# A work list recorded first and ordered by the kernel's own scheduler, with fixed buffers, fewer register loads, first transposes on the matrix engine and weight loads held to set steps

## The chip, the cores and the metric

The kernel runs on one core of a Trainium2 chip. A core has five engines that each work through an instruction list of their own, in order: TensorE (PE in the profile, with its weight loads as PEld), VectorE (DVE), ScalarE (ACT), GpSimd (POOL) and SyncE (SP). Here SP computes nothing; it issues the DMA transfers, which 16 DMA engines then carry out. The metric is the device time of one execution in microseconds (us). Before the change its median over three runs is 957.5 us (956.35 to 960.08).

## What is computed

Block-sparse attention over 4 batches, 8 heads, 768 positions and head size 64, followed by a two-layer feed-forward network (FFN) on the 3072 rows that come out. The arithmetic is carried in pairs of fp16 numbers (a high and a low part), so a product takes two or three matmuls.

```
scores = scale * np.matmul(q, k.transpose(0, 1, 3, 2))
# mask: own and neighbouring blocks of 32, first and last block,
#       and 3 sampled blocks for each block of queries
scores = np.where(mask, scores, -1000000000.0)
attn = np.exp(scores - max); attn = attn / (sum + 1e-09)
x = attn @ v                     # heads joined: 3072 x 512
h = x @ w_in                     # 512 x 2048
g = np.maximum(0.01 * h, h)
out = g @ w_out                  # 2048 x 512
```

## The kernel before

The queries of a batch are cut into 12 *tiles* T of 64 rows. Four tiles make an *item* (12 items). Within a tile each pair of heads is a *unit*: 192 units, worked on in 192 *steps* by one Python loop over `units`. The first tile of a batch (T = 0, the first and the last block) sees all 768 keys and has two *parts* for each unit; the others see 384 gathered keys. So there are 208 parts.

A unit goes through: `unit_scores` (PE L628, two query operands qs and qxs for the high and low parts), `unit_ttr` (DVE L637: mask, scale and row minimum), `unit_exp` (ACT L648), `pair_norm` (DVE L656, L657), `unit_high` (ACT L663: high half of the probabilities, pp), `unit_split` (DVE L668: low half; then a DMA transpose of pp into pt, issued on SP at L671), `pair_av` (PE L689: 24 matmuls for two parts). `tile_evac` turns a finished tile into x (ACT L698, DVE L701, ACT L707, POOL L709). When the four tiles of an item are there, its FFN work may start: 192 matmuls h (L724) and 96 matmuls o (L751), with ACT L731, DVE L735 and L740 and POOL L741 between them. The score and av matmuls use the array in another shape than the FFN's: they run as pieces of 128x64, the FFN's matmuls as 128x128.

Keys and queries are prepared by `prep_k` and `prep_q`, which end in DMA transposes on SP (L494, L517). For a tile after the first, `gather_k` copies six sampled key blocks on POOL (L573), each behind a register load (L572), and `gather_v` fetches six sampled value blocks by DMA on SP (L603), each behind a register load on SP (L601).

The weights arrive as 8-byte numbers and are decoded to fp32 and split: `load_w` (SP L286), `decode` (ACT L292, DVE L293 to L298), `finish` (PE L172 and L122, then ACT L353 and L355, POOL L356). They come in eight parts (four quarters of w_in and of w_out). The FFN of the first two items runs quarter by quarter as its weights become ready; all later items wait for the whole.

The order on each engine was made by the framework: the instructions are written in program order with a priority each (`tc.cur_priority`, 200 for each step), tile pools hand out buffers, and the framework's own list scheduler with a timeline model fixes the order. `bank` and `scale_sum` take PSUM banks from pools: two for scores, two for o, three for h and all sums, one for av. `in_order` adds order between the gathers.

Of the kernel before, what the change touches and what calls it, by code (L numbers as in the profile page):

```python
# [11 lines left out]
F16 = mybir.dt.float16  # L12
BF16 = mybir.dt.bfloat16
F32 = mybir.dt.float32
I32 = mybir.dt.int32
# [38 lines left out]
    "v_at": 28,  # L54
    "wr": [(0, 1.0), (4, 3.0), (10, 4.0), (18, 4.5)],
    "wsplit": "ppppppdd",
    "xbufs": 3,
}


@with_exitstack
def tile_block_sparse_attention_ffn(
# [19 lines left out]
    nc = tc.nc  # L82
# [17 lines left out]
    cst = ctx.enter_context(tc.tile_pool(name="cst", bufs=1))  # L100
    pw = ctx.enter_context(tc.tile_pool(name="pw", bufs=1))
    sm = ctx.enter_context(tc.tile_pool(name="sm", bufs=4))
    pa = ctx.enter_context(tc.tile_pool(name="pa", bufs=2))
    pf = ctx.enter_context(tc.tile_pool(name="pf", bufs=2))
    dr = ctx.enter_context(tc.tile_pool(name="dr", bufs=2, space=bass.MemoryType.DRAM))
    ps_s = ctx.enter_context(tc.tile_pool(name="ps_s", bufs=2, space=bass.MemoryType.PSUM))
    ps_o = ctx.enter_context(tc.tile_pool(name="ps_o", bufs=2, space=bass.MemoryType.PSUM))
    ps_1 = ctx.enter_context(tc.tile_pool(name="ps_1", bufs=1, space=bass.MemoryType.PSUM))
# [3 lines left out]

    def bank(name, tag="h"):
        return ps_1.tile([P, 512], F32, tag=tag, name=name, bufs={"h": 3, "av": 1}[tag])

# [32 lines left out]
    loose = set()  # L148

    def scales(ss, n, name, **how):  # L150
        now = tc.cur_priority
        tc.cur_priority = now - CFG["bs"]
        begin = len(nc.cur_bb.bb.instructions)
        pb = scale_sum(ss, n, name)
        loose.update(i.name for i in nc.cur_bb.bb.instructions[begin:])
        r = scale_of(pb, n, name, **how)
        tc.cur_priority = now + 8
        return r

    eye = cst.tile([P, P], BF16, name="eye")  # L160

    def squares(parts, name, fl):


        now = tc.cur_priority
        tc.cur_priority = now - CFG["bs"]
        pb = bank(f"{name}_sq")
        blocks = [t.bitcast(BF16).rearrange("p (n l) -> p n l", l=2)[:, c:c + P, 1]
                  for t in parts for c in range(0, t.shape[1], P)]
        begin = len(nc.cur_bb.bb.instructions)  # L170
        for i, t in enumerate(blocks):
            nc.tensor.matmul(pb[:, :P], t, t, start=(i == 0), stop=(i == len(blocks) - 1))  # L172
        loose.update(i.name for i in nc.cur_bb.bb.instructions[begin:])
# [3 lines left out]
        tc.cur_priority = now + 24  # L177
# [11 lines left out]
    offs = cst.tile([1, NB * NR], I32, name="offs")  # L189
    mask = cst.tile([P, NT - 1, SLOTS], F32, name="mask")  # L190

    def load_constants():
        nc.sync.dma_start(out=eye, in_=c_eye)
        nc.sync.dma_start(out=row, in_=sampled.bitcast(I32).rearrange("(o a) b -> o (a b)", o=1))
# [4 lines left out]
    def build_masks():  # L199
        nc.vector.tensor_scalar(  # L200
            out=offs, in0=row.rearrange("p (a b) -> p a b", b=2)[:, :, 0], scalar1=5, scalar2=None,
            op0=ALU.logical_shift_left)
# [17 lines left out]
        pm = bank("mask_ps")[:, :(NT - 1) * 2 * NR].rearrange("p (t a r) -> p t a r", t=NT - 1, a=2)  # L220
# [56 lines left out]
    def load_w(g):  # L277
# [8 lines left out]
        nc.sync.dma_start(out=raw.rearrange("p (c x) l -> p c (x l)", c=g.w), in_=src.bitcast(I32))  # L286

        def decode():


            lo, hi, f, d = raw[:, :, 0], raw[:, :, 1], g.d, g.d.bitcast(I32)
# [14 lines left out]
    def prep_weights():  # L306
# [33 lines left out]
        def finish(n, kind, gs):  # L340
            inv, s = scales(squares([g.d for g in gs], f"{kind}{n}", "w"), 1, f"{kind}{n}", keep=f"{kind}{n}", fl="w")
# [66 lines left out]
    def prep_v(b):  # L408
# [13 lines left out]
        scr[b] = dr.tile([S, H * 2 * D], F16, tag="scr", name=f"scr_{b}")  # L422
# [44 lines left out]
    def prep_k(b, hp, rk):  # L467

        nm = f"k{b}_{hp}"
# [30 lines left out]
    def prep_q(b, j, i, rq):  # L500

        nm = f"q{b}_{j}_{i}"
# [14 lines left out]
        nc.sync.dma_start_transpose(out=qs, in_=flat(qa))  # L517
# [22 lines left out]
    def in_order(key, begin):  # L540

        new = nc.cur_bb.bb.instructions[begin:]
        last = last_use.setdefault(key, deque())
        if len(last) > 1:
            for i in new[:-1]:
                tc.add_manual_dep(i, last[0], mybir.DependencyInfo(
                    mybir.DependencyClass.NoSync, mybir.DependencyReason.DATA), reason="order")
            last.popleft()
        last.append(new[-1].name)
# [8 lines left out]
    def gather_k(b, T):  # L558
# [11 lines left out]
        for slot, i in sampled_of(T):  # L570
            begin = len(nc.cur_bb.bb.instructions)
            off = nc.gpsimd.value_load(offs[:1, i:i + 1], min_val=0, max_val=S - BLOCK)  # L572
            nc.gpsimd.tensor_copy(  # L573
# [576 lines left out]
```

## Time and profile before

| what | us |
|---|---|
| median of three runs | 957.5 |
| span of the profiled execution | 959.4 |
| TensorE matmul busy | 775.6 (81%) |
| VectorE busy | 609.4 (64%) |
| ScalarE busy | 493.8 (51%) |
| GpSimd busy | 328.3 (34%) |
| mean share of the DMA engines' time | 67.8% |

The profiled execution's own time is its span, from the first to the last instruction; it lies 0.2% above the median of the three runs. Busy time of TensorE counts a matmul from its start to its modelled end, and matmuls overlap, so it overstates the work: 24 h matmuls that follow each other take 24 times the distance of their starts, not 24 times their length. SP's DMA issues are not counted as busy; they are shown as SPq.

### The profile page before, as it was taken

What the parts mean: (1) busy time and instruction counts of PE and PEld (TensorE: products, weight loads), DVE (VectorE), ACT (ScalarE), POOL (GpSimd) and SP (SyncE); (2) the same over time, 40 slices, a digit from 0 to 9 for tenths busy, and PEclk for the clock granted to TensorE, in tenths of its full rate; (3) what the DMA queues carried; (4) which work ended last, traced back from release to release, by engine and by line L of the source; (5) the groups of instructions that cost most, each with busy time, mean ns of one, the idle gap of its engine ahead of it and who ended that gap; (6) DMA issues with size and microseconds to landing.
All of it is one profiled execution on the core that took longest, in us unless ns stands there. A gap on an engine that the chain in (4) does not pass through costs nothing.

```text
span 959.4 us, 21885 instructions
## 1 busy us (share of the span) xinstructions
PE 775.6 (81%) x7020; PEld 485.8 (51%) x7020; DVE 609.4 (64%) x1643; ACT 493.8 (51%) x1061; POOL 328.3 (34%) x469
## 2 busy tenths in 40 slices
PE   1325445878988989997988979897989999999998
PEld 1213233535556555554655545555555655655675
DVE  4986778897576957455766556556666566655221
ACT  4564774755564646445545545555555554545121
POOL 0133544562213424423422344332423334432221
PEclk9996555999998999998999999998998999999999
DMA  9995986957767676685676868766785755556200
GB/s 212 279 269 117 271 169 141 204 113 151 152 167 147 125 147 148 147 146 122 134 175 133 161 121 144 164 135 132 162 164 104 151 135 131 119 114 124 34 23 23
DMA packets 336625, 139.39 MB, mean 145 GB/s; under 512 B 299389, under 2 KB 311678, under 8 KB 336510
## 3 DMA queue, kind: packets, MB, share of 16 engines
q1 hardware_dynamic: 336510, 137.99, 67.8%
q8 instruction: 55, 0.90, 0.4%
q14 instruction: 60, 0.49, 0.2%
HBM read 65.57 MB, written 12.58 MB: 81 GB/s over the span
## 4 chain that ended last, share of the span: by engine, by line
PE 41%; DMA 19%; DVE 16%; SPq 9%; issue 7%; ACT 7%; POOL 0%; ACTq 0%; DVEq 0%
PE h L724 17%; PE o L751 15%; DMA pt<-pp 9%; PE s L628 4%; PE av L689 4%; DVE pp L668 3%; DMA kt<-k_k 3%; DVE p L637 3%; SPq L601 2%; ACT p L648 2%; DMA qs_q<-qa_q 2%; ACT pp L663 2%; SPq L603 2%; SPq L671 2%; DMA W<-in_moe_w_in_dram 1%
## 5 line engine op out<-in xcount | busy, mean ns | idle before, releaser
L724 PE MATMUL h<-x,W 128*128 128x256 f16 x2304 | 288.0, 280 | 1.7 <-DVE k_tot L136 1.2
L751 PE MATMUL o<-W,g 128*128 128x512 f16 x1152 | 280.0, 384 | 4.8 <-DVE g L740 2.7
L724 PEld LDWEIGHTS <-W 128*128 128x128 f16 x2304 | 225.1, 101 | 52.9 <-issue 11.0
L668 DVE SCALAR_TENSOR_TENSOR pp<-p,r,pp 128x384 f16<-128x384 f32 x208 | 151.6, 737 | 128.2 <-ACT pp L663 127.5
L741 POOL TENSOR_TENSOR g<-ht,g 128x512 f16<-128x512 f32 x96 | 115.1, 1199 | 263.6 <-DVE g L740 170.7
L663 ACT ACTIVATE pp<-p,r 128x384 f16<-128x384 f32 x208 | 122.0, 608 | 143.2 <-DMA pt<-pp 111.9
L648 ACT ACTIVATE p<-p,mx 128x384 f32<-128x384 f32 x208 | 126.4, 608 | 98.2 <-DVE mx L637 61.6
L573 POOL COPY kg<-kt 128x256 f16 x264 | 128.5, 508 | 133.9 <-PE s L628 73.2
L751 PEld LDWEIGHTS <-g 128*128 128x128 f16 x1152 | 103.3, 98 | 135.0 <-issue 22.8
L689 PE MATMUL av<-pt,vg 128*64 128x128 f16 x2112 | 100.7, 231 | 47.6 <-DMA pt<-pp 44.8
L637 DVE CUSTOM_DVE_ANT_0 p<-s,em,nsc 128x384 f32<-128x384 f32 x176 | 106.1, 609 | 33.2 <-PE s L628 32.5
L689 PEld LDWEIGHTS <-vg 128*64 128x64 f16 x2112 | 79.5, 115 | 88.8 <-issue 76.4
L735 DVE SCALAR_TENSOR_TENSOR ht<-h,gd,ht 128x512 f32<-128x512 f32 x80 | 59.6, 746 | 54.8 <-ACT ht L731 54.7
L709 POOL TENSOR_TENSOR x<-xf,x 128x256 f16<-128x256 f32 x48 | 34.4, 717 | 155.8 <-ACT x L707 155.8
L731 ACT ACTIVATE ht<-h,gs 128x512 f32<-128x512 f32 x80 | 54.0, 675 | 56.2 <-PE h L724 45.2
L628 PE MATMUL s<-kg,qs_q 128*64 128x384 f16 x352 | 66.4, 368 | 17.9 <-DVE mx L637 15.1
L628 PEld LDWEIGHTS <-qs_q 128*64 128x64 f16 x416 | 27.8, 114 | 92.5 <-issue 70.4
L628 PE MATMUL s<-kg,qxs_q 128*64 128x384 f16 x352 | 63.7, 350 | 6.9 <-DMA qxs_q<-qs_q 6.9
L740 DVE CAST g<-ht 128x512 f16<-128x512 f32 x96 | 41.7, 435 | 8.9 <-PE o L751 7.8
L628 PE MATMUL s<-kt,qs_q 128*64 128x384 f16 x64 | 12.8, 396 | 35.0 <-DVE mx L637 19.7
L648 ACT ACTIVATION_READ_ACCUMULATOR p<-p,mx 128x1 f32 x208 | 39.0, 187 | 0.0
L356 POOL TENSOR_TENSOR W<-W 128x1024 f16<-128x1024 f32 x12 | 28.8, 2409 | 28.5 <-ACT W L355 22.0
(126 smaller groups left out, 727.1 us busy)
## 6 DMA issues: line engine op xcount, KB each, us to landing
vg<-scr SPq DMA_DIRECT2D x280, 64.0 KB, 1.9
vg<-scr SPq DMA_DIRECT2D x44, 256.0 KB, 3.1
v<-in_v_dram SPq DMA_DIRECT2D x32, 192.0 KB, 4.0
qxs_q<-qs_q SPq DMA_DIRECT2D x48, 128.0 KB, 2.4
scr<-v SPq DMA_DIRECT2D x16, 384.0 KB, 3.5
W<-in_moe_w_in_dram SPq DMA_DIRECT2D x5, 1024.0 KB, 7.2
rq<-in_q_dram SPq DMA_DIRECT2D x20, 256.0 KB, 3.9
out_dram<-ob SPq DMA_DIRECT2D x20, 256.0 KB, 2.8
```

The costliest lines, as they stand in the source:

```text
L573: nc.gpsimd.tensor_copy(out=kg[:, :, slot * BLOCK:(slot + 1) * BLOCK], in_=kt[:, :, bass.ds(off, BLOCK)])
L628: nc.tensor.matmul(sp[hh * D:(hh + 1) * D, :], st[:, h, c0:c0 + Q2], keys, start=(n == 0), stop=(n == 1))
L637: nc.vector.tensor_tensor_reduce(out=u.p[i], in0=u.sp[i], in1=kgs[u.b, u.T][1] if u.T else zero.to_broadcast([P, KEYS]), scale=u.nsc, scal ...
L648: nc.scalar.activation(u.p[i], u.p[i], AF.Exp, scale=-1.0, bias=u.mx[:, :1], accum_out=u.pair.sum[:, u.pi, i:i + 1])
L663: nc.scalar.activation(pp[:, 0, :], p, AF.Copy, scale=u.r)
L668: nc.vector.scalar_tensor_tensor(out=pp[:, 1, :], in0=p, scalar=u.r, in1=pp[:, 0, :], op0=ALU.mult, op1=ALU.subtract)
L689: nc.tensor.matmul(pr.av[hh * D:(hh + 1) * D, u.hp], vt[:, l * D:(l + 1) * D], u.pt[c // NCH][:, :, c % NCH, hh * D:(hh + 1) * D], start=( ...
L724: nc.tensor.matmul(c.ph[:, i], W16[:, 2 * b, d, wl, o:o + P], it.x[:, xl, d, :], start=(d == 0 and m == 0), stop=(d == NP - 1 and m == 2))
L731: nc.scalar.activation(c.t, c.ph, AF.Copy, scale=scale[1])
L735: nc.vector.scalar_tensor_tensor(out=c.t, in0=c.ph, scalar=scale[0], in1=c.t, op0=ALU.mult, op1=ALU.max)
L741: nc.gpsimd.tensor_tensor(out=c.g[:, 1], in0=c.t, in1=c.g[:, 0], op=ALU.subtract)
L751: nc.tensor.matmul(it.po[t], c.g[:, gl, i, t * P:(t + 1) * P], W16[:, 2 * (f // PER) + 1, f % PER, wl, :], start=(c.first and i == 0 and m ...
```

## The change

The kernel's calls no longer go to the framework's engines directly. `Plan` and `Engine` stand in their place: each call becomes a `Task` with an engine, a priority, a modelled cost, and the memory cells that it reads and writes. `Plan.block` joins a run of matmuls into one task that is not broken up (12 matmuls of h, 6 of o, 12 of av, 4 of scores for one part). At the end `Plan.order` runs an event model in which every engine takes the ready task with the lowest priority number, PE with a surcharge (`stay`) on a task of another array shape, and `Plan.issue` writes the instructions out in that order for the framework to keep.

Buffers are fixed rings in place of pools (`Pool`, `banks`); sums and squares go to the free last 128 columns of the two score banks (`corner`), so the three h banks hold only h. Three gathered blocks share one register load, and the values are clamped beforehand so that no bounds check stands in the queue. The transposes of the first item (four of keys, two of queries, 20 of probabilities) are done by PE against a unit matrix, with a copy out of PSUM on ACT, four of them on DVE (`turned`). A weight part's load may start only when a given step's exp has begun (`after`, `wp`, `wlead`).

```diff
+    "stay": 400.0,
+    "wp": [2, 5, 14, 17, 20, 23, 26, 29],
+    "wlead": 4,
...
+class Plan:
+    def add(self, t):
+        t.prio, t.n, t.then, t.gate = self.prio, len(self.tasks), [], self.gate
+        self.prio += 1.0
...
+        for i in need:
+            self.tasks[i].then.append(t.n)
...
+        def take(t, e):
...
+            if e == "PE":
+                best = min(ready[e], key=lambda j: tasks[j].prio + (CFG["stay"] if tasks[j].kind != mode[0] else 0.0))
+                ready[e].remove(best)
+            else:
...
+                best = heapq.heappop(ready[e])[1]
...
+    def issue(self):
+        order, self.begun = self.order()
+        with self.tc.manual_schedule():
+            for i in order:
+                for run in self.tasks[i].run:
+                    run()
...
-    nc = tc.nc
+    nc = plan = Plan(tc)
...
+    def corner():
+        buf = spare[turn["sum"] % 2]
...
+        return View(buf.ap[:, KEYS:], buf, buf.gen)
...
     def scale_sum(ss, n, name):
-        pb = bank(f"{name}_sum")
+        pb = corner()
...
+    def turned(tag, out, in_, eng):
+        n = in_.shape[1]
+        pb = bank("turn", tag).bitcast(F16)[:, :n]
+        with plan.block():
+            for c in range(0, n, P):
+                nc.tensor.transpose(pb[:, c:c + P], in_[:, c:c + P], eye16)
+        if eng == "ACT":
+            nc.scalar.activation(out, pb, AF.Copy)
+        else:
+            nc.vector.tensor_copy(out=out, in_=pb)
...
-        nc.sync.dma_start(out=raw.rearrange("p (c x) l -> p c (x l)", c=g.w), in_=src.bitcast(I32))
+        plan.prio = 1000.0 + 200 * (CFG["wp"][g.part] - CFG["wlead"])
+        with plan.after(CFG["wp"][g.part] - CFG["wlead"]):
+            nc.sync.dma_start(out=raw.rearrange("p (c x) l -> p c (x l)", c=g.w), in_=src.bitcast(I32))
...
-    def sampled_of(T):
-        return [(6 + a * NR + r, (2 * T - 1 + a) * NR + r) for a in range(2) for r in range(NR)]
+    def sampled_of(T, a, engine):
+        _, rows = tc.nc.values_load_multi_w_load_instructions(
+            offs.ap[:1, T - 1, a, :NR], engines={engine}, min_val=0, max_val=S - BLOCK,
...
-        for slot, i in sampled_of(T):
-            begin = len(nc.cur_bb.bb.instructions)
-            off = nc.sync.value_load(offs[:1, i:i + 1], min_val=0, max_val=S - BLOCK)
-            ps, c = place(slot)
-            nc.sync.dma_start(out=vg[ps, c, :], in_=scr[b][bass.ds(off, BLOCK), :])
-            in_order("v", begin)
+        for a in range(2):
+            def moves(a=a):
+                for slot, off in sampled_of(T, a, mybir.EngineType.SP):
+                    ps, c = place(slot)
+                    tc.nc.sync.dma_start(out=vg.ap[ps, c, :], in_=scr[b].ap[bass.ds(off, BLOCK), :])
...
+            if u.item.n == 0:
+                turned("o", pt.rearrange("p l c t -> p (l c t)"), pp.rearrange("p l t -> p (l t)"), "ACT")
+            else:
+                nc.sync.dma_start_transpose(
+                    out=pt.rearrange("p l c t -> p (l c) t"), in_=pp.rearrange("p l t -> p (l t)"))
```

In the changed kernel most instructions are recorded through one helper line (L384), so they are told apart by the names of what they write and read.

The first place is SP's list at the gather of values of one tile in the first batch. vg is the buffer of gathered values, scr the values in DRAM, offs the table of block offsets, pt and pp the transposed and plain probabilities. Before:

```order
L593 DMA vg_95<-scr_516 128x1024
L601 TENSOR_LOAD offs
L601 ISA x2
L603 ISA
L603 DMA vg_95<-scr_516 32x1024
L601 TENSOR_LOAD offs
L601 ISA x2
L603 ISA
L603 DMA vg_95<-scr_516 32x1024
```

And now, with the query and probability transfers that stand between the two halves:

```order
L384 DMA vg_86<-scr_71 128x1024
L982 TENSOR_LOAD offs
L1036 ISA
L1036 DMA vg_86<-scr_71 32x1024
L1036 ISA
L1036 DMA vg_86<-scr_71 32x1024
L1036 ISA
L1036 DMA vg_86<-scr_71 32x1024
L384 DMA qxs_103<-qs_102 64x1024 x2
L384 DMA_TRANSPOSE pt_140<-pp_138 128x6x128
L982 TENSOR_LOAD offs
```

One register load serves three gathers, and a transpose no longer has to stand behind all six. In all, SP has 264 loads of registers before and 88 now, and 248 transposes before and 222 now.

The second place is PE's list in the middle of the run, where the o matmuls of the FFN (o from W and g) meet the attention's av matmuls. Before, four of the twelve av matmuls of a part stand alone between two o matmuls:

```order
L751 MATMUL o_2_0_1_5437<-W,g_2_12_6406 128x512
L689 LDWEIGHTS vg_95
L689 MATMUL av_1_0_0_6470<-pt_1_0_2_0_6245,vg_95 64x128
L689 LDWEIGHTS vg_95
L689 MATMUL av_1_0_0_6470<-pt_1_0_2_0_6245,vg_95 64x128
L689 LDWEIGHTS vg_95
L689 MATMUL av_1_0_0_6470<-pt_1_0_2_0_6245,vg_95 64x128
L689 LDWEIGHTS vg_95
L689 MATMUL av_1_0_0_6470<-pt_1_0_2_0_6245,vg_95 64x128
L751 LDWEIGHTS g_2_12_6406
L751 MATMUL o_2_0_0_5430<-W,g_2_12_6406 128x512
```

Now all twelve av matmuls of a part stand together, and so do the six o matmuls of a group; this is the seam behind one such dozen:

```order
L384 LDWEIGHTS vg_86
L384 MATMUL av_70<-pt_140,vg_86 64x128
L384 LDWEIGHTS vg_86
L384 MATMUL av_70<-pt_140,vg_86 64x128
L384 LDWEIGHTS g_210
L384 MATMUL o_66<-W,g_210 128x512
```

Counted over the whole list, PE goes 506 times from attention matmuls to others or back before, and 302 times now. The counts of h, o, score and av matmuls are the same (2304, 1152, 832, 2496); 184 transposes by PE are new.

The third place is the head of SP's list. W in moe_w_in is a weight load, kt a key transpose, qs a query transpose, qxs its swapped copy, rq and v loads of queries and values. Before:

```order
L286 DMA W<-in_moe_w_in_dram 128x2x1024
L193 DMA eye<-in_eye_dram 128x128
L194 DMA tmps<-in_sampled_blocks_dram 1x144
L195 DMA allow<-in_allow_dram 24x24
L196 DMA iota<-in_iota_dram 24x24
```

And now, from the last loads of values on:

```order
L384 DMA v_108<-in_v_dram 128x6x64
L384 DMA qxs_103<-qs_102 64x1024 x2
L384 DMA v_108<-in_v_dram 128x6x64
L384 DMA W<-in_moe_w_in_dram 128x2x1024
L384 DMA kt_83<-in_moe_w_in_dram 128x2x1024
```

The first weight load moved from ahead of the constants to behind all loads of queries, keys and values of the first batch, and no transpose stands on SP before the one for the queries of the second item.

More of the change, by code (lines that the diff above doesn't have):

```diff
@@ L1 @@
+import heapq
 from collections import deque
-from contextlib import ExitStack
+from contextlib import ExitStack, contextmanager
+from itertools import count
 import ml_dtypes
@@ new lines, with cells @@
+SIZE = {F16: 2, BF16: 2, F32: 4, I32: 4}
+def cells(view):
+    ap = view.ap
+    size = SIZE[ap.dtype]
+    if ap.space == bass.MemoryType.DRAM:
+        return {(ap.name,)}
+    row = int(np.prod(ap.tensor.shape[1:]))
+    grain = 4 if row * size <= 640 else 64
+    dims = list(ap.ap)
+    p0, at = divmod(ap.offset, row)
+    parts = range(p0 // BLOCK, (p0 + dims[0][1] - 1) // BLOCK + 1)
+    starts = np.array([at * size])
+    run = size
+    free = [(s * size, n) for s, n in dims[1:] if n > 1 and s]
+    while free and free[-1][0] <= max(run, grain):
+        run = (free[-1][1] - 1) * free[-1][0] + run
+        free.pop()
+    for s, n in free:
+        starts = (starts[:, None] + np.arange(n)[None, :] * s).ravel()
+    pieces = set()
+    for a in starts:
+        pieces.update(range(int(a) // grain, (int(a) + run - 1) // grain + 1))
+    return {(ap.name, p, c) for p in parts for c in pieces}
@@ new lines, with elements, run_bytes @@
+class Task:
+    __slots__ = ("eng", "run", "busy", "late", "reads", "writes", "prio", "kind", "loads", "need", "then", "n", "gate")
+COST = {
+    "wake": {"PE": 100, "DVE": 25, "ACT": 60, "POOL": 90, "SP": 17},
+    "change": {("a", "f"): 140, ("f", "a"): 95},
+    "lanes": 8,
+    "fly": 1250,
+    "land": 400,
+    "slice": 200,
+}
+def elements(ap):
+    return int(np.prod([n for _, n in list(ap.ap)[1:]] or [1]))
+def run_bytes(ap):
+    size = SIZE[ap.dtype]
+    dims = list(ap.ap)[0 if ap.space == bass.MemoryType.DRAM else 1:]
+    n = 1
+    for s, c in reversed([d for d in dims if d[1] > 1]):
+        if s != n:
+            break
+        n *= c
+    return n * size
@@ L110, in tile_block_sparse_attention_ffn @@
+    def corner():
+        buf = spare[turn["sum"] % 2]
+        turn["sum"] += 1
+        buf.gen += 1
+        return View(buf.ap[:, KEYS:], buf, buf.gen)
+    scrs = [Buffer(dram.tile([S, H * 2 * D], F16, name=f"scr{i}")) for i in range(2)]
     zero = cst.tile([P, 1], BF16, name="zero")
     nc.vector.memset(zero, 0.0)
-    def bank(name, tag="h"):
-        return ps_1.tile([P, 512], F32, tag=tag, name=name, bufs={"h": 3, "av": 1}[tag])
     ones = cst.tile([P, P], F32, name="ones")
@@ L538, in tile_block_sparse_attention_ffn @@
     last_use = {}
[L540 to L549, printed above, removed]
-    def sampled_of(T):
-        return [(6 + a * NR + r, (2 * T - 1 + a) * NR + r) for a in range(2) for r in range(NR)]
+    def sampled_of(T, a, engine):
+        _, rows = tc.nc.values_load_multi_w_load_instructions(
+            offs.ap[:1, T - 1, a, :NR], engines={engine}, min_val=0, max_val=S - BLOCK,
+            skip_runtime_bounds_check_because="the block numbers are clamped to the sequence before they are shifted")
+        return zip(range(6 + a * NR, 6 + (a + 1) * NR), rows)
     kgb = [pa.tile([P, H, KEYS], F16, tag=f"kg{i}", name=f"kg{i}", bufs=1) for i in range(2)]
@@ L954, in tile_block_sparse_attention_ffn @@
     units = [u for it in items for u in it.units]
+    for n, u in enumerate(units):
+        u.n = u.pair.n = n
     live = [0]
@@ L990, in av_step @@
                 vfree[0] += pr.T > 0
-                evs.append(tile_evac(pr))
+                evs.append((pr.n, tile_evac(pr)))
     def ev_step():
-        if evs and next(evs[0], "end") == "end":
-            evs.pop(0)
+        if evs:
+            with plan.level(evs[0][0] + CFG["pr"][7]):
+                end = next(evs[0][1], "end") == "end"
+            if end:
+                evs.pop(0)
     for u in units:
```

463 lines of the change are left out of this document (393 added, 70 removed).

## The prediction

> **What bounds the kernel now.** I read the busy table first, then the stages, then what PE waits for in each, then SP's issues.
>
> ```profile
> PE 775.6 (81%) x7020; PEld 485.8 (51%) x7020; DVE 609.4 (64%) x1643; ACT 493.8 (51%) x1061; POOL 328.3 (34%) x469
> ```
>
> PE is the fullest engine. Five stretches of the span (columns: stretch and length, then busy us and instructions of PE, PEld, DVE, ACT, POOL, then granted clock, DMA share, GB/s) show where it isn't full:
>
> ```profile
> 0.00:72.00 72.00, 17.83 (x102) 11.42 (x104) 52.66 (x152) 38.24 (x66) 13.18 (x21) 1.00 1.09 253
> 72.00:168.00 96.00, 46.00 (x460) 32.16 (x458) 72.97 (x174) 58.04 (x110) 40.57 (x47) 0.59 0.75 174
> 168.00:240.00 72.00, 57.57 (x538) 36.36 (x535) 63.39 (x178) 43.39 (x93) 33.48 (x42) 0.93 0.74 157
> 240.00:860.00 620.00, 560.10 (x5184) 345.10 (x5183) 390.89 (x1084) 328.11 (x744) 219.91 (x339) 0.97 0.69 142
> 860.00:959.00 99.00, 94.05 (x757) 60.76 (x753) 29.52 (x61) 25.97 (x49) 21.12 (x20) 1.00 0.27 54
> ```
>
> The reader is to see three stages: a **start** of 240 us with PE busy for 121.4, a **middle** of 620 us with PE idle for 59.9, and a **tail** in which the FFN alone fills PE. The tail's order is the same in both kernels (312 h and 180 o matmuls stand behind the last scores in each list), so I leave it at 99 us.
>
> Busy PE overstates the work. What one matmul takes in an unbroken run comes from the chain of waits and the timeline (start, length, what, count):
>
> ```profile
> 906.86 0.79 PE av L689 x24
> 939.92 2.62 PE h L724 x24
> 942.54 2.59 PE o L751 x12
> 311.12 0.33 PE L628 MATMUL s<-kg,qs_q 128*64 128x384 f16 x2
> 311.29 0.33 PE L628 MATMUL s<-kg,qxs_q 128*64 128x384 f16 x2
> 311.55 2.79 PE L724 MATMUL h<-x,W 128*128 128x256 f16 x24
> 314.27 0.35 PE L628 MATMUL s<-kg,qs_q 128*64 128x384 f16 x2
> ```
>
> So h takes 2.62/24 = 0.109 us, o 0.216, av 0.033, and a score matmul 0.085 (two start 0.17 after the two ahead). The last score pair would be over at 311.46, and h starts at 311.55; 24 h end at 314.17, and scores start at 314.27: a change of shape costs **0.09 to 0.1 us**. The counts in the middle (for h, o, scores, av in this order):
>
> ```profile
> 240.00:860.00 620.00, 219.34 (x1750) 168.74 (x1747) 0.97 0.69 142
> 240.00:860.00 620.00, 214.93 (x876) 77.75 (x876) 0.97 0.69 142
> 240.00:860.00 620.00, 84.15 (x632) 27.38 (x632) 0.97 0.69 142
> 240.00:860.00 620.00, 85.90 (x1866) 67.61 (x1868) 0.97 0.69 142
> ```
>
> 1750 x 0.109 + 876 x 0.216 + 632 x 0.085 + 1866 x 0.033 = 191 + 189 + 54 + 62 = 496 us; at the granted 0.97 that is 511. The middle holds 632 of 832 score matmuls, 76%, so some 385 of the 506 changes of shape, 37 us. 511 + 37 = 548 of the 560 busy; the rest is small. The middle is therefore 548 of work, some 12 unexplained, 60 idle.
>
> **Middle: SP's list.** What PE idles for is seen around 505 us (PE, SP and again PE rows of the timeline):
>
> ```profile
> 504.46 0.35 PE L628 MATMUL s<-kt,qxs_q 128*64 128x384 f16 x2
> 512.51 2.58 SPq L671 DMA_TRANSPOSE pt<-pp  x2
> 516.16 4.76 SPq L603 DMA_DIRECT2D vg<-scr  x5
> 521.40 2.68 SPq L671 DMA_TRANSPOSE pt<-pp  x2
> 525.67 0.53 PE L689 MATMUL av<-pt,v 128*64 128x128 f16 x12 [0.81 <-DMA pt<-pp]
> PE av L689 <- DMA pt<-pp: 24.8, 22, 2.8
> ACT pp L663 <- DMA pt<-pp: 86.6, 52, 4.5
> ```
>
> The last two transposes of a unit were issued at 521.40, behind five gathers that hold the list for 4.76 us, and PE waited for them. The last two rows are the sums over the middle (us, times, longest) of PE's and ACT's waits for such a transpose. What the gathers cost there (rows of the queue: min/median/max ns, and a gather in the timeline):
>
> ```profile
> L601 SPq TENSOR_LOAD <-offs x264: 263/273/871, 27.3 to 887.9; - x132
> L601 SPq FUSED_REGOPS  x264: 152/152/184, 27.8 to 888.3; - x132
> L603 SPq DMA_DIRECT2D vg<-scr x264: 315/316/993, 72.9 to 888.7; - x132
> 588.56 0.58 SPq L593 DMA_DIRECT2D vg<-scr  x1
> 590.15 5.89 SPq L603 DMA_DIRECT2D vg<-scr  x6
> 596.15 5.24 SPq L671 DMA_TRANSPOSE pt<-pp  x4
> SPq L671 <- PE s L628: 14.9, 21, 1.7
> SPq L435 <- ACT v L428: 0.2, 1, 0.2
> 240.00:860.00 620.00, 108.99 (x318) 0.97 0.69 142
> ```
>
> A tile's gather holds SP from 588.56 to 596.15, 7.6 us, some 1.1 for each of six. The last row is ACT's exp in the middle, two instructions for a part, so 159 parts. The two rows ahead of it are the first and the last of the 48 groups of SP's own waits there; they add up to 108 us, so SP is at work for 512 of 620, 83%, in strict order, with 7.6 us lumps. Now a triple costs a load and three DMAs. A DMA alone takes 0.32 plus some 0.1 of register work and gaps; a load of three values is not in the trace: between one load's 0.27 and three loads' 0.82, and I take 0.5. Triple: 0.5 + 3 x 0.42 = 1.8 against 3.3; two triples save 3.1 us for a tile, 2.4 at the worse end. The 159 parts make some 40 tiles: SP falls from 512 to about 390, 63%, and the lump is halved, with transposes between. POOL loses the same loads, but it is 35% busy, which gives nothing.
>
> The Trainium skill ("DMA: Bandwidth & Descriptors", Latency and other measured facts) has a floor of some 600 ns for such a load; the trace differs, at 0.273. By 0.6 the estimate for two triples would save 2.9 instead of 3.1, and the sum stands.
>
> PE in the middle: 302 changes of shape instead of 506, by the same share 230 x 0.095 = 22 instead of 37: **-15**. The 12 unexplained stay. Of the 60 idle I let SP's relief take 38: the 25 that av waits for pt, and 13 of the 35 left, since late transposes also hold buffers that ACT waits for (86.6 us) and with it the scores behind; ends 0 and 55. **Middle -53**, from -15 to -70.
>
> **Start.** The FFN can begin when x of the first four tiles is there (POOL's rows of x, then the first h):
>
> ```profile
> 99.37 0.67 POOL L709 TENSOR_TENSOR x<-xf,x 128x256 f16<-128x256 f32 x1 [2.12 <-ACT x L707]
> 158.82 0.88 POOL L709 TENSOR_TENSOR x<-xf,x 128x256 f16<-128x256 f32 x1 [4.73 <-ACT x L707]
> 162.07 0.37 PE L724 MATMUL h<-x,W 128*128 128x256 f16 x1
> 149.68 0.85 PE L689 MATMUL av<-pt,vg 128*64 128x128 f16 x12 [3.63 <-DMA pt<-pp]
> 158.02 0.85 PE L689 MATMUL av<-pt,vg 128*64 128x128 f16 x12 [4.74 <-DMA pt<-pp]
> L415 ACT ACTIVATE v<-v 128x768 f16<-128x768 f32 x16 | 13.4, 834 | 6.4 <-DMA v<-in_v_dram 6.3
> W<-in_moe_w_in_dram SPq DMA_DIRECT2D x5, 1024.0 KB, 7.2
> ```
>
> The first and the fourth x lie 59 us apart, 20 for a tile, and PE's waits in it end with a DMA transpose. The change takes these 26 transposes off SP (some 35 us of issue at 1.3 each) and off DMA engines that are full to 72 us (1.09), where weights no longer come first. It adds 184 PE transposes: none in the trace, from 0.03 (av, same 128 columns) to 0.11 (h), so 6 to 20 us, under PE's 118.6 idle. ACT gets 24 copies of 768 columns and two of 1024, some 22 us by its 768-column square (0.834), under 100 idle. If that cover goes, each is in the chain of its unit, one us for a part. DVE gets four, 4 us.
>
> What is late next is DVE: 52.7 + 73.0 + 63.4 = 189 us of decoding, attention and FFN in 240, 79%. I let it run at 92%: (189 + 4)/0.92 = 210, **-30**. Ends: 0 if the holding back of weights eats it, and -45 at DVE 99%.
>
> Holding back: parts 2 to 7 load four steps ahead of their decoding. A weight load lands in 7.2 us by the last row, and the start has 44 parts (208 less 159 and the tail's 5) in 240 us, over five us each, so four steps cover it twice. Cost 0.
>
> A rule speaks against the PE transposes: the Trainium skill ("TensorE: Matmul & The Clock Gate", Part 4) says that transposes there do not count as activity for the clock. The granted 0.59 between 72 and 168 shows that sparse work does lower the clock. By the rule the start would stay there and the FFN begin some 10 us later, an estimate, for -20 in place of -30.
>
> **The sum.** 959.4 - 53 - 30 = 876; the profiled run lies 1.9 above the median, so **874.5**.
>
> **Rivals.**
> 1. *PE becomes solid* (0.15): idle in the middle falls to 5 and DVE fills the start: 959.4 - 70 - 45 - 2 = 842, and to 825 if the 12 unexplained go too. For it: work of 548 in 620. Against: PE still waits in order.
> 2. *The wait moves* (0.18): transposes still come late, since DVE and ACT chains are as long; the middle gives only the changes of shape and ten us of idle, the start ten: 959.4 - 25 - 10 - 2 = 922; 905 to 950.
> 3. *No change* (0.04): the list says the same thing otherwise. Behind 128 parts of scores both lists have 1104 h matmuls, so coarse pacing is equal; but the start and the seams differ. 957.
> 4. *Slower, lead too short* (0.11): in PE's list the work between a part's scores and its av is, at the durations above, 24.8 us in the median of the middle before, and 15.4 now, about 2.2 pairs of units. If a part's way through DVE, ACT, SP and DMA takes longer than that, PE waits in order with the FFN behind it. A pair takes 620/79 = 7.8 us now, so it decides at 2.2 x 7.8 = 17 us of way; at 20 us a pair would take 9.1, and 79 pairs cost 100 more, less 30 from the start: 1025. The row at 504.46 and its av at 525.67 have 21 us of way, with the lumps in it; without the lump of 5 and without waits for av it is nearer 13, which is why I give it little.
>
> **Chances.** Forecast 0.52 (850 to 905), the others as above. Faster by over 0.5% 0.85, within 0.5% 0.04, slower 0.11; half a per cent is about what a measurement of this kernel can tell from no change. The range of 8 in 10 runs from **828 to 938**: it leaves out the slower case, no change and the outer parts of rivals 1 and 2.
>
> **What would show it.** Right: PE's wait of av for pt in the middle falls below 10 us, the lump of a gather is near 4 us, the fourth x stands before 130 us, PE idles below 30 in the middle. Wrong: first h still near 160 us (start); av waits more than 25 us for pt in the middle (rivals 2 and 4); h broken by waits on x or W; a triple load of over a us on SP.

## The result, and the profile after

The changed kernel takes **923.3 us** in the median of five runs (921.33 to 927.57), against 958.8 (956.35 to 961.28) for the kernel before on the same chip: a ratio of 0.9636, 95% interval 0.9607 to 0.9666. Faster, as forecast, but by 35 us where the forecast was 83. The profiled spans are 925.9 and 959.4.

The page's busy table of the changed kernel:

```profile
PE 767.3 (83%) x7204; PEld 499.0 (54%) x7204; DVE 626.3 (68%) x1650; ACT 509.4 (55%) x1087; POOL 330.0 (36%) x469
```

The span less the busy time is PE's idle time: 183.8 us before, 158.6 now. So PE is busy 8.3 us less and idle 25.2 us less. The stretches of the changed kernel, by the columns used before:

```profile
72.00:168.00 96.00, 62.93 (x614) 43.38 (x614) 81.74 (x177) 67.58 (x122) 47.54 (x49) 0.71 0.69 192
168.00:240.00 72.00, 59.64 (x518) 38.56 (x519) 67.41 (x183) 43.48 (x91) 28.21 (x38) 0.87 0.76 166
240.00:860.00 620.00, 549.40 (x5394) 352.59 (x5393) 412.57 (x1111) 338.23 (x773) 224.05 (x345) 0.99 0.73 149
```

The middle idles for 70.6 us, where it was 59.9 before and was to fall below 30. A stretch between fixed times holds other work in each kernel. It is better cut by work: from the end of the 48th part's scores to the end of the last. That is 248 to 883 us before (all engines, then h and o alone):

```profile
248.00:883.00 635.00, 574.36 (x5324) 353.96 (x5320) 397.45 (x1097) 335.85 (x763) 221.74 (x341) 0.97 0.69 141
248.00:883.00 635.00, 225.26 (x1800) 0.97 0.69 141
248.00:883.00 635.00, 220.51 (x900) 0.97 0.69 141
```

and 250 to 847 us in the changed kernel (its 48th part's scores end at 247.4; the twelve o matmuls behind them are counted to the start):

```profile
250.00:847.00 597.00, 527.12 (x5173) 338.92 (x5174) 398.09 (x1071) 326.06 (x748) 217.73 (x338) 0.99 0.74 151
250.00:847.00 597.00, 204.35 (x1704) 0.99 0.74 151
250.00:847.00 597.00, 205.19 (x853) 0.99 0.74 151
```

The middle is 38 us shorter; the start (248 and 250) and the tail (76.4 and 78.9) are not. In the middle stand 96 h and 47 o matmuls fewer, 96 x 0.109 + 47 x 0.216 = 20.6 us. They are done elsewhere: the start has 72 h and 36 o more (15.6 us), and the tail 24 h and 12 o more (5.2 us; one o lies on the cut). The rows of h behind the last scores, before and now:

```profile
883.00:959.40 76.40, 32.93 (x288) 1.00 0.14 33
847.00:925.90 78.90, 36.04 (x312) 1.00 0.10 27
```

Of the 47.2 us of busy time that the middle lost, the other 47.2 - 20.6 = 26.6 went away, and idle time rose by 9.2 (60.6 to 69.9). What PE waits for from 240 to 860 us now (us, times, longest):

```profile
PE av L384 <- DMA vg<-scr: 29.6, 20, 2.7
PE av L384 <- DMA pt<-pp: 25.0, 29, 2.3
PE s L384 <- DMA qxs<-qs: 4.4, 4, 1.4
PE s L384 <- DVE mx L384: 4.1, 5, 2.2
```

The wait of av for its transpose has not moved (24.8 before), and **a new wait for the gathered values** stands beside it. The timeline at 553 us shows how it comes about (start, length, what, count):

```profile
551.02 1.23 SPq L384 DMA_TRANSPOSE pt<-pp  x1
553.63 1.34 SPq L1036 DMA_DIRECT2D vg<-scr  x3
554.53 0.41 PE L384 MATMUL av<-pt,vg 128*64 128x128 f16 x8
555.02 0.42 SPq L384 DMA_DIRECT2D rq<-in_q_dram  x1
556.63 0.64 PE L384 MATMUL av<-pt,vg 128*64 128x128 f16 x16 [1.69 <-DMA vg<-scr]
```

PE begins on a tile's av 0.9 us after SP has begun to issue its last three gathers, and then stands for 1.69 us. SP itself did become cheaper, as the rows of its loads and the first and last group of its own waits (29 groups, 165.8 us in all from 240 to 860) show:

```profile
L982 SPq TENSOR_LOAD <-offs x88: 664/690/1141, 83.5 to 845.2; - x88
SPq L384 <- PE s L384: 34.6, 40, 2.4
SPq L384 <- ACT ht L384: 0.2, 1, 0.2
```

SP is at work for 454 of 620 us, 73%, after 83% before. The start's own marks, the fourth x and the first h:

```profile
124.48 0.66 POOL L384 TENSOR_TENSOR x<-xf,x 128x256 f16<-128x256 f32 x1
125.69 2.53 PE L384 MATMUL h<-x,W 128*128 128x256 f16 x11
```

### The profile page after: what moved, and what is told of

Read it like the earlier page. It is cut to its first block, busy times and chain, and to the rows that moved or that the text cites. A ratio compares the mean times of both kernels' runs of the same rounds, so it can differ in the third digit from the quotient of the medians.

```text
span 925.9 us, 20826 instructions
## 1 busy us (share of the span) xinstructions
PE 767.3 (83%) x7204; PEld 499.0 (54%) x7204; DVE 626.3 (68%) x1650; ACT 509.4 (55%) x1087; POOL 330.0 (36%) x469
## 5 line engine op out<-in xcount | busy, mean ns | idle before, releaser
L384 PEld LDWEIGHTS <-W 128*128 128x128 f16 (+1 forms) x2480 | 237.8, 101 | 83.6 <-DVE W L384 24.5
L384 PE MATMUL o<-W,g 128*128 128x512 f16 x1152 | 278.1, 388 | 4.0 <-DVE g L384 2.8
L384 PE MATMUL h<-x,W 128*128 128x256 f16 x2304 | 278.4, 276 | 3.0 <-ACT x L384 2.1
L384 POOL TENSOR_TENSOR g<-ht,g 128x512 f16<-128x512 f32 x96 | 117.1, 1220 | 285.0 <-DVE g L384 207.0
L384 PEld LDWEIGHTS <-g 128*128 128x128 f16 x1152 | 109.6, 100 | 132.5 <-issue 21.0
L384 DVE SCALAR_TENSOR_TENSOR pp<-p,r,pp 128x384 f16<-128x384 f32 x208 | 147.6, 738 | 45.6 <-ACT pp L384 45.1
L384 ACT ACTIVATE p<-p,mx 128x384 f32<-128x384 f32 x208 | 125.8, 606 | 91.9 <-DVE mx L384 91.2
L384 ACT ACTIVATE pp<-p,r 128x384 f16<-128x384 f32 x208 | 118.8, 606 | 75.4 <-DMA pt<-pp 26.8
L384 PE MATMUL av<-pt,vg 128*64 128x128 f16 x2112 | 90.5, 228 | 54.5 <-DMA vg<-scr 29.6
L384 DVE SCALAR_TENSOR_TENSOR ht<-h,gd,ht 128x512 f32<-128x512 f32 x80 | 59.9, 749 | 106.3 <-ACT ht L384 105.8
L384 DVE CUSTOM_DVE_ANT_0 p<-s,em,nsc 128x384 f32<-128x384 f32 x176 | 104.7, 609 | 31.6 <-PE s L384 30.6
L384 ACT ACTIVATE ht<-h,gs 128x512 f32<-128x512 f32 x80 | 54.5, 681 | 118.4 <-PE h L384 110.7
L384 PEld LDWEIGHTS <-vg 128*64 128x64 f16 x2112 | 71.8, 114 | 88.4 <-issue 70.2
L384 PE MATMUL s<-kg,qs 128*64 128x384 f16 x352 | 64.0, 354 | 15.9 <-DVE mx L384 14.0
L384 POOL TENSOR_TENSOR x<-xf,x 128x256 f16<-128x256 f32 x48 | 35.9, 747 | 96.2 <-ACT x L384 96.0
L384 PE MATMUL s<-kg,qxs 128*64 128x384 f16 x352 | 63.5, 349 | 4.7 <-DMA qxs<-qs 4.7
L384 PEld LDWEIGHTS <-qs 128*64 128x64 f16 x416 | 29.2, 114 | 40.9 <-issue 32.0
L384 DVE CAST g<-ht 128x512 f16<-128x512 f32 x96 | 42.5, 443 | 10.8 <-PE o L384 6.5
L384 ACT ACTIVATION_READ_ACCUMULATOR p<-p,mx 128x1 f32 x208 | 39.1, 188 | 0.0
L384 DVE TENSOR_SCALAR sum<-sum 128x2 f32<-128x2 f32 x96 | 28.5, 297 | 15.3 <-ACT p L384 14.7
L384 POOL TENSOR_TENSOR W<-W 128x1024 f16<-128x1024 f32 x12 | 28.1, 2349 | 27.9 <-ACT W L384 25.6
```

Source lines behind the costliest of these rows:

```text
L384: self.plan.task(self.eng, lambda: f(*a, **k), busy, late, reads, writes, kind, loads)
```

## The experiments

Two theories stood against each other. **The lead**: the new order puts the av of a part too shortly behind its scores, and PE, which works in order, stands there for whatever of transposes and gathers comes last. **The load**: the gain and the rest are set by single costs (SP's loads, the gather's place, the DMA's latency, changes of shape), each to be found alone. All runs are in one table, in the order of the text. "Changes" are changes of array shape in PE's list, "lead" is the work in that list between a part's scores and its av (parts 48 to 195, median, at the durations of the prediction), "av waits" is how long av waits for pt and vg from 250 to 840 us (both in us), busy and idle are PE's over the profiled span, and the ratio is to the kernel before.

| run | changes | lead | av waits | busy | idle | ratio, 95% |
|---|---|---|---|---|---|---|
| before | 506 | 24.3 | 23.9 | 775.6 | 183.8 | 1 |
| after | 302 | 15.9 | 54.0 | 767.3 | 158.6 | 0.9636 (0.9607 to 0.9666) |
| e1 | 342 | 15.7 | 44.0 | 773.1 | 157.1 | 0.9699 (0.9681 to 0.9717) |
| e2 | 302 | 15.9 | 54.6 | 776.1 | 160.0 | 0.9767 (0.9739 to 0.9794) |
| e3 | 286 | 15.0 | 43.9 | 750.7 | 174.7 | 0.9619 (0.96 to 0.9638) |
| e4 | 434 | 14.4 | 52.6 | 783.2 | 159.5 | 0.9807 (0.9791 to 0.9824) |
| e5 | 314 | 14.6 | 47.1 | 771.7 | 144.4 | 0.9601 (0.956 to 0.9641) |
| e6 | 316 | 16.9 | 43.9 | 768.4 | 165.8 | 0.9708 (0.9667 to 0.9749) |
| e7 | 284 | 17.0 | 39.1 | 759.2 | 150.1 | 0.9519 (0.9481 to 0.9557) |
| e8 | 424 | 23.9 | 10.4 | 764.0 | 163.2 | 0.9698 (0.9642 to 0.9753) |
| e9 | 230 | 17.8 | 24.2 | 761.7 | 143.5 | 0.9492 (0.9453 to 0.9531) |
| e14 | 222 | 21.0 | 28.4 | 757.5 | 156.5 | 0.9573 (0.9528 to 0.9617) |
| e11 | 284 | 17.0 | 44.5 | 769.6 | 154.8 | 0.9649 (0.9599 to 0.97) |
| e10 | 266 | 17.1 | 34.8 | 748.9 | 166.6 | 0.9526 (0.9486 to 0.9567) |
| e16 | 384 | 18.7 | 22.1 | 778.9 | 131.4 | 0.9513 (0.9475 to 0.9551) |
| e17 | 438 | 15.6 | 25.5 | 766.4 | 169.0 | 0.9821 (0.9787 to 0.9856) |

The expectations of e14, e16 and e17 give other leads (19 for after, 31 or 32 for before): they put 0.2 us on every FFN matmul. The table's column replaces them; the order of the kernels is nearly the same in both.

**e1, the gathers of values ranked earlier.**

```diff
-        gather_v(b, T)
+        with plan.level(b * NT * NP + T * NP - 4):
+            gather_v(b, T)
```

> The changed kernel, with the gather of a tile's values ranked four steps ahead of the tile's first unit. The changed kernel stands at 0.964 of before, and av waits 29.6 us for the gathers. Theory A (the gathers are put on SP just in time, and that wait is new): the wait falls below 8 us, PE idles 20 us less in the middle, ratio to before 0.940 to 0.946. Theory B (the attention's chain sets the pace, the wait only moves to the transposes): av's wait for pt grows by about what the other loses, ratio 0.960 to 0.968.

Measured: 931.3 us. The wait for vg is gone from the middle, and the wait for pt has taken its place (PE's waits from 250 to 840 us):

```profile
PE av L384 <- DMA pt<-pp: 44.0, 39, 3.4
PE s L384 <- DVE mx L384: 3.7, 7, 1.0
```

So 20 of the 30 us came back as a wait for pt: which transfer is late goes with what stands ahead on SP. The edit also brings 40 changes of shape, and the 48th part's scores end 8 us later than in after, so its ratio alone decides little; the moved wait does.

**e2, one register load for each gather again, on SP and on POOL, in the same order.** The bounds checks of the kernel before stay out.

```diff
-        _, rows = tc.nc.values_load_multi_w_load_instructions(
-            offs.ap[:1, T - 1, a, :NR], engines={engine}, min_val=0, max_val=S - BLOCK,
...
+        for r in range(NR):
+            _, rows = tc.nc.values_load_multi_w_load_instructions(
+                offs.ap[:1, T - 1, a, r:r + 1], engines={engine}, min_val=0, max_val=S - BLOCK,
...
+            yield 6 + a * NR + r, rows[0]
```

> The changed kernel with one register load for each gather again (264 loads each on SP and POOL), the order of every engine unchanged. Theory A (SP's relief was a part of the gain): a tile's gather gets 1.5 to 2 us longer on SP, 44 tiles, and PE waits for it in order: ratio 0.985 to 1.000. Theory B (SP has slack in the new order): the same SP time is added and nothing waits for it, ratio 0.962 to 0.970.

Measured: 937.9 us, 0.013 above after in the ratio and between the two. The edit puts back only a part of what SP was relieved of. Where the six gathers of a tile stand in one row of SP's queue, they take 5.94 us in the median before (23 rows), 3.69 in after and 4.66 here, so 6.4, 4.4 and 4.9 with the first load ahead of them. The same tile in after and in this run:

```profile
468.99 3.62 SPq L1036 DMA_DIRECT2D vg<-scr  x6
472.96 4.67 SPq L1037 DMA_DIRECT2D vg<-scr  x6
```

What stays away is the bounds check: before, each load is followed by register work of 0.152 us (the prediction shows its row) and by

```profile
L601 SPq SEQ_ASSERT  x264: 18/18/28, 28.1 to 888.5; - x132
```

Beside after, the profile shows 8.8 us more of busy PE and only 1.4 more of idle, with the same instructions in the same order. In stretches of 20 us, after has four at a granted 0.91 between 260 and 840, this run nine at 0.91 and two at 0.94 and 0.97. Two of this run's:

```profile
260.00:280.00 20.00, 17.79 (x165) 11.07 (x166) 13.29 (x37) 9.80 (x24) 5.34 (x5) 0.91 0.87 161
320.00:340.00 20.00, 17.05 (x183) 11.64 (x182) 8.15 (x22) 7.22 (x18) 7.24 (x11) 0.91 0.63 134
```

A stretch at 0.91 loses 1.8 us at most; five more of them and the two others make up to 10.8, which would cover the 8.8 of this execution. That the clock is the cause is not shown: another execution of this kernel had a mean granted clock of 0.936 and took 938.08 us, while those of after had 0.932 to 0.939 and took 921 to 928. Why half a microsecond more for a tile costs 10 us or more in all stays open; POOL's loads were split by the same edit, and the two were not separated.

**e3, the first item's transposes by DMA** (the three conditions that choose PE are set so that DMA does them).

```diff
-            if u.item.n == 0:
+            if False:
                 turned("o", pt.rearrange("p l c t -> p (l c t)"), pp.rearrange("p l t -> p (l t)"), "ACT")
```

> The changed kernel with the first item's 26 transposes done by DMA again. Theory A (the transposes by PE bring the early start of the FFN): the first h moves from 126 us to 145 or later and the time grows by 10 to 25 us, ratio 0.975 to 0.990. Theory B (VectorE bounds the start, 93% busy from 120 to 240 us): the first h may move, the time by less than 5 us, ratio 0.960 to 0.969.

Measured: 923.9 us, the same as after; first h at 128.1 instead of 125.7. PE is busy 16.6 us less and idle 16.1 more. The transposes on PE fill idle time and shorten nothing that shows in the time.

**e4, no surcharge on a change of shape.**

```diff
-    "stay": 400.0,
+    "stay": 0.0,
```

> The changed kernel without the surcharge on a task of another array shape: 434 changes of shape in PE's list instead of 302. Theory A (each costs some 0.095 us of PE time): 132 x 0.095 = 12.5 us more, ratio 0.974 to 0.980. Theory B (they fall into time in which PE idles anyway): less than 4 us, ratio 0.960 to 0.968.

Measured: 941.4 us, 0.017 above after in the ratio, for 132 more changes. Busy PE rises by 15.9 and idle by 0.9:

```profile
PE 783.2 (83%) x7204; PEld 495.6 (53%) x7204; DVE 621.9 (66%) x1650; ACT 510.3 (54%) x1087; POOL 328.5 (35%) x469
```

If all of it is due to the changes, 15.9/132 is **0.12 us for a change**, a little above the 0.09 to 0.1 seen in single rows. It is an estimate: in e2 busy time moved by 8.8 us without any more changes.

**e5, weight loads not held back.**

```diff
-        with plan.after(CFG["wp"][g.part] - CFG["wlead"]):
+        with plan.after(None):
```

> The changed kernel with weight loads free to start as soon as their buffer is free, at the same rank as now. Theory A (holding them back keeps DMA free for the start): the first h moves from 126 us to 135 or later, 5 to 15 us more, ratio 0.969 to 0.980. Theory B (the start is bound by VectorE, and nothing of the gain is due to it): less than 4 us, ratio 0.960 to 0.968.

Measured: 918.3 us; first h at 118.7. The interval overlaps with that of after: holding back gives nothing that shows.

**e6, the planner counts 1 us more until a DMA has landed.**

```diff
-    "land": 400,
+    "land": 1400,
```

> The changed kernel, whose scheduler now takes a DMA to land one us later (1400 ns instead of 400). Only the order changes. Theory A (the order is drawn up tight to a model in which transfers land too early, so PE, in order, waits 54 us in the middle for transposes and value gathers): these waits fall below 30 us and the ratio to 0.940 to 0.955. Theory B (the waits are a pace of the attention's chain and only change their names): waits of 45 to 60 us, ratio 0.958 to 0.970.

Measured: 928.7 us. Av's waits fall by 10 only (in an execution of 936 us, the slowest of the four), and no time is gained; the ratio is 0.007 above after. The waits are not cured by a longer figure for one latency.

**e7, av and the eviction of a tile ranked two steps later.**

```diff
-    "pr": [-1, 0, 0, 0, 0, 0, 0, 0],
+    "pr": [-1, 0, 0, 0, 0, 0, 2, 2],
```

> The changed kernel with the av matmuls and the work behind them ranked two steps later. Theory A (PE takes av too early): av's waits fall from 54 us below 35, ratio 0.948 to 0.958. Theory B (av later holds the transposed tiles and the value buffers longer, and the wait moves there): ratio 0.962 to 0.975.

Measured: 910.6 us. Busy and idle both fall by some 8 us; av's waits fall from 54 to 39.

**e8, the kernel before with one register load on SP for three gathers of values, and without the bounds check of each value**, and nothing else of the change; the framework still makes the order.

```diff
-        for slot, i in sampled_of(T):
+        for a in range(2):
...
-            off = nc.sync.value_load(offs[:1, i:i + 1], min_val=0, max_val=S - BLOCK)
...
+            _, rows = nc.values_load_multi_w_load_instructions(
+                offv[:1, T - 1, a, :NR], engines={mybir.EngineType.SP}, min_val=0, max_val=S - BLOCK,
+                skip_runtime_bounds_check_because="the block numbers are drawn inside the sequence")
+            for slot, off in zip(range(6 + a * NR, 6 + (a + 1) * NR), rows):
```

> The kernel before with one register load on SP for three value gathers, alone; its order is again made by the framework and has 424 changes of shape instead of 506. The prediction's theory (SP's list is what PE idles for in the middle): idle of PE in the middle falls by 25 or more, ratio 0.945 to 0.970. Theory B (SP's loads are worth what the single loads cost the changed kernel, 13 us, and the shape changes their share of 11): 0.972 to 0.985, with idle nearly as before. Theory C (nothing): 0.996 to 1.004.

Measured: 927.3 us: a ratio of 0.9698, where the whole change has 0.9636. **This edit alone gives 29 us of the 35.** PE's waits from 250 to 840 us:

```profile
PE o L759 <- DVE g L748: 12.6, 8, 3.0
PE av L697 <- DMA pt<-pp: 10.4, 10, 2.6
PE s L636 <- DVE mx L645: 6.5, 8, 1.6
```

The wait for pt falls from 23.9 to 10.4, and idle in the middle, cut by work (229.6 to 851.7 us here), from 60.6 to 46.6. That is what the prediction had in mind, at a third of its size. The framework's order also comes out with 82 changes of shape fewer, about 10 us at 0.12, which is nearly all of the 11.6 us of busy time that went.

**e9 and e14, av four and six steps later.**

```diff
-    "pr": [-1, 0, 0, 0, 0, 0, 0, 0],
+    "pr": [-1, 0, 0, 0, 0, 0, 4, 4],
```

> After with av and the eviction of a tile ranked four steps later instead of two (0.9519). 230 changes of shape against 284. Theory A (the lead of a part's scores over its av is what PE lacks, and each further step of it takes waits away): av's waits in the middle fall from 39 to about 25 us, the changes of shape give another 5 to 7, ratio 0.930 to 0.938. Theory B (the lead is not it; the transposes and gathers are late in any order since SP and the rings of buffers hold them): av's waits stay at 35 to 45, and only the changes of shape come out, 0.944 to 0.948. Theory C (a longer lead fills the rings of probabilities, scores and FFN wait instead): 0.952 or more, with waits of the scores in place of av's.

> The same with six steps. 222 changes of shape, and in PE's list the work between a part's scores and its av is in the median of parts 100 to 180 near 28 us at the trace's durations, against 19 in after, 21 with two steps and 31 in the kernel before. Theory A: av's waits 15 us or less, PE idle in the middle 35 or less, ratio 0.915 to 0.930. Theory B: av's waits 35 to 45, ratio 0.943 to 0.948. Theory C: scores or FFN wait, ratio 0.955 or more.

Measured: 908.7 and 917.0 us. With four steps av's waits are down to 24.2, as expected of the lead; the time is not (0.9492 where 0.930 to 0.938 was expected), since other waits come up (PE's waits of e9 from 250 to 840 us):

```profile
PE av L384 <- DMA pt<-pp: 13.0, 13, 4.4
PE s L384 <- DVE mx L384: 11.7, 12, 2.8
PE av L384 <- DMA vg<-scr: 11.2, 7, 3.4
PE s L384 <- ACT k L384: 4.2, 4, 1.4
```

With six steps the scores wait more, for queries that ACT and DMA bring (16.6 us, 5.7 in e9), and PE idles 13 us more: 9 of them in the middle, 4 behind the last scores. Of the ranks tried, four steps are the best, and the waits as a whole don't vanish with it.

**e11, e7 with one register load for each gather**, by the edit of e2.

> The kernel with av two steps later, with one register load for each gather again, in the same order on every engine. Theory A (SP's time is still what the waits come from; the longer lead has not covered it): about 13 us dearer as without the longer lead, ratio 0.963 to 0.969. Theory B (the lead covers the loads now): 0.951 to 0.957.

Measured: 925.3 us, 0.013 above e7 in the ratio; in the profile 10.4 us more are busy and 4.7 idle. The longer lead has not covered the loads.

**e10, e7 without holding back and without the transposes on PE**, by the edits of e5 and e3.

> Av two steps later, weight loads not held back, and the first item's transposes by DMA, which leaves the triple loads, the own order and the fixed rings of the change. 266 changes of shape against 284. Theory A (transposes by PE and the holding back are worth nothing, alone and together): 0.945 to 0.955. Theory B (they carry the start together: without both the DMA queues delay the first tiles, first h at 140 us or later): 0.960 to 0.975.

Measured: 912.9 us, the same as e7, though the first h comes only at 149.8 us, 20 later than in e7. By the end of the 48th part's scores (241.6 us, 244.4 in e7) both have nevertheless done 288 h matmuls.

**e16, e4 with av four steps later, and e17, e8 with av no longer written three steps late**, to separate the lead from the changes of shape.

```diff
-    "av_lag": 3,
+    "av_lag": 0,
```

> The new order without the surcharge on changes of shape, with av and the eviction ranked four steps later: 384 changes of shape against 434 in the run without the surcharge alone (0.9807), and in PE's list a lead of scores over av of 22 us in the median of parts 100 to 180 against 17. Theory A (the short lead is what the new order pays with): av's waits in the middle, 54 us there, fall to 25 to 30, and with 50 changes at 0.137 the ratio comes to 0.953 to 0.963. Theory B (the lead is not it): only the changes, 0.972 to 0.976, av's waits above 45.

> The kernel before with one register load on SP for three gathers (0.9698, PE idle 46 us in the middle, 10 of them av behind transposes), and av no longer written three steps behind its probabilities: the lead of scores over av in PE's list falls from 32 us to 20 in the median of parts 100 to 180, as in the new order (19), with 438 changes of shape against 424. Theory A: av's waits come up to 30 or more, PE idle to 60 or more, ratio 0.980 to 0.990. Theory B (the lead is not it): 14 changes more are 2 us, ratio 0.967 to 0.975.

Measured: 911.0 and 938.5 us. e16 is 0.029 below e4 in the ratio, with the lead 18.7 instead of 14.4; of the 32.4 us between the spans 4.3 are busy PE (50 changes) and **28 are idle**. Its PE waits from 250 to 840 us:

```profile
PE av L384 <- DMA vg<-scr: 19.9, 12, 3.5
PE s L384 <- DMA qxs<-qs: 4.5, 4, 1.9
PE av L384 <- DMA pt<-pp: 2.2, 4, 0.8
```

e17 does the reverse in the old order: lead 23.9 to 15.6, and the wait is back:

```profile
PE av L697 <- DMA pt<-pp: 25.5, 23, 3.1
PE s L636 <- DMA kt<-k_k: 8.6, 1, 8.6
```

It is 0.012 dearer than e8 (8.2 us between the profiled spans), within the range of theory A, but not for its reason: the middle idles for 46.1 us where e8 has 46.6, since other waits shrank as this one grew. The loss is in the start, where the 48th part's scores end at 249.8 us instead of 229.6. So a short lead brings this wait back, and e17 does not show that the lead costs time in the middle.

## Why the prediction was right in sign and wrong in size

**The failed step is "Of the 60 idle I let SP's relief take 38".** PE's idle time in the middle rose by 9 us instead. That is a miss of 47, as much as the whole error of 50 in the span (876 forecast, 925.9 measured); the errors of the other terms nearly cancel. The runs split the miss in two:

- **The relief is worth less.** SP is at work for 73% of the middle now, after 83%. In the old order (e8), with the same 73%, this takes 14 us off the middle's idle time (60.6 to 46.6), not 38.
- **The new order spent it.** Against e8 it idles 23 us more (69.9). Most of that comes back when av is ranked later: 49.7 us in e9, and 45.6 in e16 against 67.3 in e4. PE leads the rows of after, e8 and e9 from 250 to 840 us:

```profile
250.00:840.00 590.00, 520.12 (x5101) 334.22 (x5101) 394.35 (x1061) 323.14 (x741) 216.57 (x337) 0.99 0.74 151
250.00:840.00 590.00, 543.50 (x5098) 340.49 (x5095) 381.70 (x1067) 322.38 (x735) 215.36 (x337) 0.97 0.72 147
250.00:840.00 590.00, 540.26 (x5323) 359.32 (x5321) 398.46 (x1092) 329.91 (x757) 220.65 (x343) 0.98 0.76 153
```

The prediction credited the relief to a kernel whose order it had just described as shorter in lead, 15.4 us of work between scores and av after 24.8. It gave this a rival of its own with a threshold: slower if a part's way is over 17 us, free if below. There was no such cliff, and it was not free. Av waited 54 us for its inputs in after, and 39, 24 and 22 in e7, e9 and e16, with leads of 17.0, 17.8 and 18.7. That the lead is the measure of it is not shown: e1, e3 and e5 have leads of 14.6 to 15.7, shorter than after's 15.9, and waits of 44 to 47, and e14 waits 28.4 us at 21.0. What is shown is that the rank of av in the new order decides these waits. The other parts of the new order (matmuls joined into blocks, fixed rings, sums in the score banks) were not undone one by one.

The other terms:

- **Changes of shape, -15 forecast.** Too small: 26.6 us of busy time went from the middle. 0.12 us a change (e4) on 204 fewer is 24.5 us, some three quarters of it in the middle, and the granted clock there went from 0.97 to 0.99, which was not in the sum. The two together would cover the 26.6; their shares were not measured apart. The count was right, and the price may be a fifth too low.
- **Start, -30 forecast.** Some 14: by the cut it ends 2 us later (250 after 248), with 15.6 us more of h and o done. The fourth x came at 124.5 us, under the 130 that was to show the step right. The reason given was wrong: e3 has the transposes on DMA and e10 a first h at 150 us, and neither is dearer than the kernel it is to be compared with. The first h is a mark, not a bound. That the new order and the triple loads share the gain is likely, since e8 alone has its 48th part at 229.6 us (with 23 h and 24 o fewer done, 7.7 us), but it wasn't separated.
- **DVE late next, at 92%.** Only in the last third, with 67.41 of 72 us from 168 to 240, 94%. Over the first 250 us DVE is busy for 208.7, 83%, and the start did not shorten to 210. That DVE sets its length is not shown.
- **PE transposes and holding back, 0 forecast.** Right: e3, e5 and e10. The transposes were put at 6 to 20 us of PE; without them (e3) PE is busy 16.6 us less, and their groups (busy, mean ns, then idle ahead of them), where matmuls overlap, list 23.8:

```profile
L384 PE MATMUL o<-eye,pp 128*128 128x128 f16 x120 | 16.0, 297 | 18.5 <-ACT pp L384 9.9 <-DVE pp L384 7.6 <-ACT pt L384 0.9
L384 PE MATMUL h<-eye,W 128*128 128x128 f16 x48 | 6.1, 312 | 9.5 <-DVE W L384 5.7 <-DVE eye L384 3.8
L384 PE MATMUL o<-eye,qa 128*128 128x128 f16 x16 | 1.7, 268 | 1.2 <-DVE qa L384 1.2
```

By the rule of the Trainium skill ("TensorE: Matmul & The Clock Gate", Part 4) the start would have given 20 in place of 30, and some 14 came. The trace does not agree on the reason: the granted clock of the first 120 us is 0.68 with them and 0.78 without (e3), but the time is the same. Nor do the prediction's rows show that sparse work lowers the clock: the sparser stretch from 0 to 72 us, with PE busy for 17.83, was granted 1.00.

- **The triple load, 0.5 us assumed.** 0.690 measured. By the rows with all six gathers (e2), a tile takes 6.4 us of SP's list before and 4.4 now. It saves 2.0 us instead of 3.1, less than the 2.4 of the worse end. SP's demand came to 454 us in the 620, for 164 parts, not 390 for 159.
- **The 12 unexplained us and the tail, unchanged.** The tail grew by 2.5. Its order is not the same in both kernels: 288 h and 168 o matmuls stand behind the last scores before, and 312 and 180 now. The 12 us stay unexplained.
- **Rival 2** named the time (922), by luck: it let idle time fall by ten where it rose by 9, and took the changes of shape at 15. Its wait that moves is seen in e1, where the wait for vg goes and the wait for pt grows by 20. **Rival 4** named av's short lead, but as a cliff; ranking av later bears out the direction.

The sum by measured terms: -26.6 (busy time gone) - 20.6 (matmuls moved out of the middle) + 9.2 (idle) + 2 (length of the start) + 2.5 (tail) = -33.5, which is 959.4 to 925.9.

What remains open: why single loads cost 10 us or more of PE's time (e2, e11), why SP's relief takes only 14 us, and which of the other waits keep PE's idle time in the middle at 45 to 50 us, in e8, e9, e16 and e17 alike. Several kernels beat both: e9 at 0.9492, with e16, e7 and e10 within its interval. All of them rank av later.

## What to carry to other kernels

Relief on a queue is worth only what the new order leaves of the wait behind it: when a change both shortens transfers and moves consumers nearer to their producers, price the two together, and don't take the second as free below a threshold. Give consumers of late transfers a later rank before looking for better latencies (e7, e9 and e16 against e6). And undo single parts: here one edit of a few lines (e8) gave 29 us, where a rewritten scheduler with it gave 35.

## What the runs showed of the hardware

- A register load of three values takes 0.690 us on SP and 0.740 on POOL in the median; one of a single value took 0.273 on SP. The price goes mostly by the value, not by the load: three single loads are 0.82 us, so joining them saves 0.13. The bounds check that went with them was dearer: 0.152 and 0.018 us for each value, 0.51 for three. The Trainium skill ("Runtime: NRT & Kernel Launch", Instruction fetch mechanics) gives some 200 ns for a register of a TENSOR_LOAD; the rows agree, with (0.690 - 0.273)/2 = 0.21.
- The granted clock of a whole execution does not order the times: e9, the quickest kernel, had 0.919 to 0.928 in its four executions, and one of e2 took 938.08 us at 0.936. In the profiled executions e2 and e11 have 9 to 10 us more of busy PE than after and e7, with the same instructions in the same order, and more 20-us stretches at 0.91 from 260 to 840 us (9 against 4, and 9 against 2). That a slower queue brings these about is not shown.
- A change of array shape costs some 0.11 to 0.12 us of PE's busy time, an estimate from two pairs of runs (e4 against after, and e16 against e9 with 17.2 us for 154). Yet e16 is as quick as e9, since it idles less (131.4 us against 143.5): the surcharge that saves the changes seems to take away work that would fill PE's idle time.
